# Attention's products with v, from the second query tile on, as float32 with one head in each half of the array's columns

## The chip, the cores and the metric

One core of a Trainium2 chip runs the whole kernel. The metric is the device time of one execution in microseconds. The engines are named as the profile names them: PE (TensorE's matmuls), PEld (its weight loads), DVE (VectorE), ACT (ScalarE), POOL (GpSimd) and SP (the engine whose queue issues most DMAs).

## What is computed

Windowed attention with a distance bias feeds a mixture of four experts, and that feeds one more two-layer network. Cut to what matters:

```python
# q, k, v: (2, 8, 576, 64) float32
scores = np.matmul(q, k.transpose(0, 1, 3, 2)) / np.sqrt(64)
mask = (rel >= 0) & (rel < 128)                  # rel = query - key
scores = np.where(mask, scores + bias, -1e9)     # bias = -slope[h] * |rel|
attn = softmax(scores)
x = np.matmul(attn, v)                           # -> (1152, 512), heads side by side
for e in range(4):                               # w1: 512 x 1024, w2: 1024 x 512
    out += p[:, e:e + 1] * (np.maximum(x @ w1[e], 0) @ w2[e])
h = np.maximum(out @ w_in, 0)                    # w_in: 512 x 2048
return h * h @ w_out
```

## The kernel before

**Rounded products.** Most GEMMs keep float32 accuracy by splitting each operand into a part rounded to float32r (suffix h, written by the helper `rounded`, L519 on ACT or L521 on DVE) and the remainder (suffix l, helper `rest`, L525 on POOL or DVE). A product is then three matmuls: h by h, h by l, l by h. Some early products skip the split and run on plain float32 operands.

**Units.** Attention is cut into units. One unit is a pair of heads c (of four pairs). The first four units take query tile 0 of both batches. The other 16 take one batch and two query tiles: 1 and 2 (256 queries, 384 keys), or 3 and 4 (192 queries, 320 keys, the last block of which has 64). A unit loads q, k and v (tiles rq, rk, rv), splits q and k (qh, ql, khl), and for each query tile does a job: scores (sc, L839), bias and minimum (L852), exponentials (L861), the sums and their reciprocals (L868, L872), scaling of the probabilities in ts (L883, on POOL), four transposes into PSUM (tp, L895), and a copy to SBUF (pt).

**The product with v.** In the first four units pv (L744) multiplies plain float32: each head has 64 columns of v, so its matmul uses 64 of the array's 128 columns, and its result goes to its own 64 partitions of xps. In the other 16 units the probabilities are split: `hi` copies tp to pt rounded, `lo` (DVE) writes the remainder. v is split as well into vh and vl, in fixed tiles that two units in turn share. Then for each of three key blocks pv (L759) runs three matmuls with v of both heads (128 columns) as the weights and the probabilities of both heads side by side as the moving operand:

```python
for l_, r_ in ((wh_, hi), (wh_, lo), (wl_, hi)):
    nc.tensor.matmul(
        out=xps[:, :, o0:o0 + w], lhsT=l_, rhs=r_,
```

Half of that output is of no use (head a's weights with head b's probabilities). `evh` and `evl` take the two useful quarters, 64 partitions by nq columns each, into xh and xl, the split input of the experts.

**Order.** Everything up to 24 items of the first expert's GEMMs is one plan. `Plan.run` is a list scheduler that runs when the program is built: a task has engines to choose from, each with an occupation and a latency, a due time, the tasks it depends on (deps) and the buffers it takes and holds (SLOTS counts the buffers of a kind). It takes the candidate that can start first, and among those that can start within 0.15 of it on the same engine the one with the earliest due time. So a change of a task's cost or its deps can reorder every engine's queue up to the plan's end. `keep_busy` puts small dummy matmuls where the plan sees PE idle near the start. PE's order in the plan mixes the attention units with the first expert's first GEMM (hps, 12 matmuls an item, L974; float32 L1758) and its second (yacc, L1210; float32 L1709). What follows the plan is written out in program order: the rest of expert 0 (hps with 384 columns, L974), then the other experts and the last network (L1093, L1184).

Of the kernel before, what the change touches and what calls it, by code (L numbers as in the profile page):

```python
# [8 lines left out]
F32 = mybir.dt.float32  # L9
F32R = mybir.dt.float32r  # L10
# [6 lines left out]
P = 128  # L17
# [114 lines left out]
def kernel(  # L132
# [346 lines left out]
    def last_runs(nt):  # L479
# [14 lines left out]


    SLOTS = dict(
        rq=3, rk=2, rv=2, qh=2, ql=2, khl=2, vp=2, sc=2, tp=2, ts=5, st=5, pt=2, work=2, y=2, h=4
    )
    plan = Plan(SLOTS)
    actx = ExitStack()  # L500
# [8 lines left out]
    def ps_tile(kind, shape, name):  # L509
        pool = psum[kind][0]  # L510
        psum[kind].append(psum[kind].pop(0))
        return pool.tile(shape, F32, tag=kind, name=name)
# [4 lines left out]
    def rounded(eng, out, in_):  # L517
        if eng == "ACT":
            nc.scalar.activation(out=out, in_=in_, func=ACTF.Copy)  # L519
        else:  # L520
            nc.vector.tensor_copy(out=out, in_=in_)  # L521

    def rest(eng, out, in0, in1):
        e = nc.gpsimd if eng == "POOL" else nc.vector
        e.tensor_tensor(out=out, in0=in0, in1=f32(in1), op=ALU.subtract)  # L525


    def act(n, lat=0.1):
        return ("ACT", 0.1 + 0.00083 * n, 0.1 + 0.00083 * n + lat)

    def dve(n, lat=0.05):
        return ("DVE", 0.15 + 0.00105 * n, 0.15 + 0.00105 * n + lat)

    def gps(n, lat=0.05):
        return ("POOL", 0.2 + 0.0021 * n, 0.2 + 0.0021 * n + lat)

    def pe(us):
        return ("PE", us, us + 0.25)
# [4 lines left out]
    def keep_busy(place):  # L543


        early = plan.at["PE"] < 1.0 and plan.gap > 2.0
        lead, each = (0.6, 0.11) if early else (-0.2, 0.08)
        for _ in range(int(max(plan.gap + lead, 0.0) / each)):
            nc.tensor.matmul(
                out=place, lhsT=idle, rhs=idle, start=True, stop=True, skip_group_check=True  # L550
            )
# [29 lines left out]
                )  # L581

    VS = 3
    vpad = []
    for i in range(2):
        vh = abias.tile([P, VS, 2, D], F32R, name=f"vh{i}")
        vl = abias.tile([P, VS, 2, D], F32R, name=f"vl{i}")
        vpad.append((vh, vl))


    units = [dict(bs=(0, 1), t0=0, t1=1, c=c, col=0) for c in range(NP)]
    for t0, t1, col, n in ((1, 3, 256, 256), (3, 5, 768, 192)):
# [14 lines left out]
    def unit_tasks(u, due):  # L607
# [8 lines left out]


        raw = t0 == 0
        b_ = {k: Buf(k) for k in ("rq", "rk", "rv", "qh", "ql", "khl", "vp", "pt", "work")}
        prev = {k: task.get((k, u - 1)) for k in ("vl", "pv", "evl")}  # L620

        def add(key, opts, fn, **kw):
            task[key, u] = plan.add(f"{key}{u}", opts, fn, **kw)
            return task[key, u]
# [40 lines left out]
        def kl(eng):  # L665
            t = b_["khl"].tile
            rest(eng, t[D:P], b_["rk"].tile, t[0:D])

        parts = [
            (slice(0, r), slice(s0, s1))  # L670
            for r, s0, s1 in ((P, 0, nb * full), (left, full, full + 1)) if r
        ]

        def vsrc():
            return b_["rv"].tile.rearrange("p k (a d) -> p k a d", a=2)

        def vh(eng):
            d["vp"] = vpad[u % 2]
            for r, k in parts:
                rounded(eng, d["vp"][0][r, k], vsrc()[r, k])  # L680

        def vl(eng):
            for r, k in parts:
                rest(eng, d["vp"][1][r, k], vsrc()[r, k], d["vp"][0][r, k])

        end = due[-1]
        first = due[0]
        kbytes = nb * 2 * D * 4 / 1024.0
# [9 lines left out]
        if not raw:  # L698
            tqh = add("qh", [act(G * nq), dve(G * nq)], qh, shared=True, deps=[lq], takes=[b_["qh"]],
                      bufs=[b_["rq"]], due=first - 9.0)  # L700
            tkh = add("kh", [act(G * nk), dve(G * nk)], kh, shared=True, deps=[lk], takes=[b_["khl"]],
                      bufs=[b_["rk"]], due=first - 9.1)
            tql = add("ql", [gps(G * nq), dve(G * nq)], ql, shared=True, deps=[tqh], takes=[b_["ql"]],
                      bufs=[b_["rq"], b_["qh"]], due=first - 8.2)
            tkl = add("kl", [dve(G * nk), gps(G * nk)], kl, shared=True, deps=[tkh],
                      bufs=[b_["rk"], b_["khl"]], due=first - 8.3)
            nv = nb * nk
            tvh = add("vh", [act(nv), dve(nv)], vh, shared=True, deps=[lv], takes=[b_["vp"]],
                      bufs=[b_["rv"]], due=end - 3.4)
            tvl = add("vl", [gps(nv), dve(nv)], vl, shared=True, deps=[tvh], bufs=[b_["rv"], b_["vp"]],  # L710
                      due=end - 2.6)

        split = []
        wide = 0
# [22 lines left out]
        def pv(eng):  # L737

            if raw:
                xps = b_["work"].tile = ps_tile("work", [P, nb * nq], "xps")  # L740
                keep_busy(xps[:, 0:P])
                for i in range(nb):
                    for a in range(2):
                        nc.tensor.matmul(  # L744
                            out=xps[a * D:(a + 1) * D, i * P:(i + 1) * P],
                            lhsT=first_in["v"][:, i, (2 * c + a) * D:(2 * c + a + 1) * D],
                            rhs=b_["pt"].tile[:, 2 * i + a, :], start=True, stop=True,
                            skip_group_check=True,
                        )
                if c == NP - 1:  # L750
                    free.extend(first_buf)
                return
            xps = b_["work"].tile = ps_tile("work", [P, G, nq], "xps")
            keep_busy(xps[:, 0, 0:P])
            for i, (k, r, p0, g, o0, w) in enumerate(mm):
                wh_, wl_ = (x[0:r, k].rearrange("p g d -> p (g d)") for x in d["vp"])
                hi, lo = (b_["pt"].tile[0:r, part, :, p0:p0 + w] for part in range(2))
                for l_, r_ in ((wh_, hi), (wh_, lo), (wl_, hi)):
                    nc.tensor.matmul(  # L759
                        out=xps[:, :, o0:o0 + w], lhsT=l_, rhs=r_,  # L760
                        start=(i == 0 and l_ is wh_ and r_ is hi),
                        stop=(i == len(mm) - 1 and l_ is wl_), skip_group_check=True,
                    )

        cols = slice(d["col"], d["col"] + nb * nq)
# [10 lines left out]
            rest(eng, xl[:, c, cols], first_x[0][0][:, c, :], xh[:, c, cols])  # L776
            x_done()

        heads = [slice(a * D, (a + 1) * D) for a in range(2)]

        def evh(eng):
            for a, hs in enumerate(heads):
                rounded(eng, xh[hs, c, cols], b_["work"].tile[hs, a, :])

        def evl(eng):
            for a, hs in enumerate(heads):
                rest(eng, xl[hs, c, cols], b_["work"].tile[hs, a, :], xh[hs, c, cols])

        us = sum(3 * max(0.112, 0.0135 + 2 * w / 2400.0) for *_, w in mm)
        tpv = add("pv", [pe(0.84 if raw else us)], pv, deps=split + ([lv] if raw else [tvh, tvl]),  # L790
                  takes=[b_["work"]], bufs=[b_["pt"]] + ([] if raw else [b_["vp"]]),
                  due=end - 1.3, follow=[prev["pv"]])
        if raw:
            add("evx", [act(nb * nq), dve(nb * nq)], evx, deps=[tpv], bufs=[b_["work"]],
# [3 lines left out]
            add("evl", [gps(nb * nq), dve(nb * nq)], xl_later, shared=True, deps=[teh],  # L798
                due=end + 7.0)
            return  # L800
        def twice(o):
            return (o[0], 2 * o[1], o[1] + o[2])

        teh = add("evh", [twice(act(nq)), twice(dve(nq))], evh, deps=[tpv], bufs=[b_["work"]],
                  due=end - 0.9)
        add("evl", [twice(dve(nq))], evl, deps=[teh], bufs=[b_["work"]], due=end - 0.4)

    def job_tasks(u, i, t, add, b_, end, ready, G, q0, k0, pos, wide):
        c = units[u]["c"]
# [93 lines left out]
            parts = [(r, k * n, n) for k, r in enumerate(rows)]  # L903

        def hi(eng):
            if raw:
                t_ = b_["pt"].tile = a_tile("pt", [P, 2, 8 * P], F32R).rearrange(
                    "p s w -> p (s w)"
                )[:, 0:G * n].bitcast(F32).rearrange("p (g w) -> p g w", g=G)
                rounded(eng, t_, s["tp"].tile)  # L910
                return
            if i == 0:
                b_["pt"].tile = a_tile("pt", [P, 2, 8 * P], F32R)[:, :, 0:G * wide].rearrange(
                    "p s (g w) -> p s g w", g=G
                )
            for r, o, m in parts:
                rounded(
                    eng, b_["pt"].tile[0:r, 0, :, pos + o:pos + o + m],
                    s["tp"].tile[0:r, :, o:o + m],
                )  # L920

        def lo(eng):
            pt_ = b_["pt"].tile
            for r, o, m in parts:
                rest(
                    eng, pt_[0:r, 1, :, pos + o:pos + o + m], s["tp"].tile[0:r, :, o:o + m],
                    pt_[0:r, 0, :, pos + o:pos + o + m],
                )

        tb = [task["bias", c, True]] + ([task["bias", c, False]] if t else [])  # L930
# [15 lines left out]
        m = G * len(cols) * n  # L946
        thi = stage("hi", [act(m), dve(m)], hi, 2.0, deps=[ttp],
                    takes=[b_["pt"]] if i == 0 else [], bufs=[s["tp"]] + ([b_["pt"]] if i else []))
        if raw:
            return [thi]  # L950
        tlo = stage("lo", [dve(m)], lo, 1.5, deps=[thi], bufs=[s["tp"], b_["pt"]])
        return [thi, tlo]

    state = {}

# [993 lines left out]
```

## Time and profile before

| | before |
|---|---|
| median of 3 runs | 660.81 us (660.63 to 661.75) |
| profiled execution, span from first to last instruction | 658.4 us |
| PE busy | 649.9 us (99%), 3953 matmul records |
| DVE busy | 486.8 us (74%) |
| ACT busy | 320.4 us (49%) |
| POOL busy | 401.7 us (61%) |
| share of PE in the chain that ended last | 89% |
| share of PE xps L759 in it | 3% |

The profile gives the profiled execution's own time only as its span; the runs' times also hold what lies before the first and after the last instruction. A busy PE is one with a matmul in flight; a matmul's record lasts longer than the time after which the next one can start, so costs are read from one row's start to the next row's start. A float32 matmul leaves two records in the trace. The attention units with rounded products lie between 19 and 137 us.

### The profile page before, as it was taken

The numbers are of one execution on the slowest core, as the hardware profiler recorded it, in microseconds if no ns is written. First come the engines' busy times: TensorE is split into PE (matmuls) and PEld (weight loads), VectorE is DVE, ScalarE is ACT, GpSimd is POOL, SyncE is SP. The second block draws the span as 40 slices with busy tenths as digits, with TensorE's granted clock in tenths as the row PEclk, the third lists the DMA queues.
The fourth block names the chain that finished last, engine by engine and source line by source line (L and its number), as shares of the span: only waits on it lengthen the run. The fifth ranks groups of instructions, "written<-read, shape, count | busy, mean of one in ns | idle before, by whom it ended". The sixth has DMA issues, their size and how long they took to land.

```text
span 658.4 us, 11199 instructions
## 1 busy us (share of the span) xinstructions
PE 649.9 (99%) x3953; PEld 582.9 (89%) x3953; DVE 486.8 (74%) x1057; ACT 320.4 (49%) x802; POOL 401.7 (61%) x488
## 2 busy tenths in 40 slices
PE   8999999999999999999999999999999999999998
PEld 7879988889898898998989989989989899898896
DVE  6998977748888768777877876867686676757563
ACT  6998877624454343443344434336545443433320
POOL 1799976509876653654654564445686786665521
PEclk9999999999999999999999999999999999999999
DMA  9952221031313344334334244231113323001012
GB/s 233 271 146 82 65 77 51 11 97 65 109 51 113 128 128 145 127 124 147 100 128 160 80 143 147 81 127 65 34 33 114 126 82 112 1 16 49 1 65 80
DMA packets 44167, 64.44 MB, mean 98 GB/s; under 512 B 4176, under 2 KB 26448, under 8 KB 44112
## 3 DMA queue, kind: packets, MB, share of 16 engines
q1 hardware_dynamic: 32704, 39.22, 19.5%
q10 hardware_dynamic: 11408, 24.51, 11.8%
q8 instruction: 31, 0.51, 0.3%
q14 instruction: 24, 0.20, 0.1%
HBM read 52.97 MB, written 10.75 MB: 97 GB/s over the span
## 4 chain that ended last, share of the span: by engine, by line
PE 89%; POOL 4%; ACT 3%; issue 2%; DMA 2%; DVE 1%; SPq 0%; POOLq 0%; ACTq 0%
PE yacc L1184 34%; PE hps L1093 31%; PE yacc L1210 7%; PE hps L974 6%; PE xps L759 3%; PE tp L895 2%; PE sc L839 2%; POOL hmem L525 1%; PE hps L1758 1%; DMA w<-wconv 1%; ACT ts L861 1%; POOL wl L525 1%; DMA first<-in_qT_dram 1%; PE xtp L1276 1%; POOL ls L525 1%
## 5 line engine op out<-in xcount | busy, mean ns | idle before, releaser
L1184 PE MATMUL yacc<-wh,hmem 128*128 128x512 f32 x716 | 227.8, 390 | 0.0
L1184 PEld LDWEIGHTS yacc<-wh,hmem 128*128 128x128 f32 x716 | 134.5, 188 | 27.1
L1184 PE MATMUL yacc<-wl,hmem 128*128 128x512 f32 x358 | 139.7, 390 | 0.0
L525 POOL TENSOR_TENSOR wl<-wraw,wh 128x256 fp32r<-128x256 f32 (+1 forms) x83 | 79.7, 985 | 39.9 <-ACT wh L458 27.9
L525 POOL TENSOR_TENSOR hmem<-c,hmem 128x320 fp32r<-128x320 f32 (+1 forms) x64 | 59.3, 945 | 60.4 <-ACT hmem L1124 60.4
L525 POOL TENSOR_TENSOR ls<-wsum,hs 128x256 fp32r<-128x256 f32 x77 | 62.1, 834 | 53.2 <-ACT hs L403 52.5
L1104 ACT ACTIVATE p<-hps 128x256 f32<-128x256 f32 (+1 forms) x80 | 32.9, 411 | 108.9 <-PE hps L1093 108.8
L1108 DVE TENSOR_TENSOR u<-hps,p 128x256 f32<-128x256 f32 (+1 forms) x80 | 36.5, 456 | 65.8 <-PE hps L1093 62.8
L1184 PEld LDWEIGHTS yacc<-wl,hmem 128*128 128x128 f32 x358 | 67.3, 188 | 12.5
L525 POOL TENSOR_TENSOR la<-wraw,ha 128x256 fp32r<-128x256 f32 x54 | 49.2, 932 | 17.3 <-ACT ha L389 17.3
L296 DVE SCALAR_TENSOR_TENSOR wconv<-wraw,wconv 128x512 int32<-128x512 int32 x64 | 57.6, 899 | 1.3
L1128 ACT ACTIVATE hmem<-c 128x256 fp32r<-128x256 f32 (+1 forms) x72 | 31.2, 445 | 52.5 <-DVE c L1108 50.7
L1129 DVE SCALAR_TENSOR_TENSOR hmem<-c,hmem 128x256 fp32r<-128x256 f32 (+1 forms) x72 | 42.5, 612 | 14.1 <-ACT hmem L1128 12.7
L1124 ACT ACTIVATE hmem<-c 128x320 fp32r<-128x320 f32 (+1 forms) x64 | 27.3, 446 | 52.4 <-DVE c L1118 33.5
L1093 PE MATMUL hps<-ht,ls 128*128 128x320 f32 (+1 forms) x160 | 47.5, 297 | 1.2 <-POOL ls L525 1.2
L1093 PE MATMUL hps<-ht,hs 128*128 128x320 f32 (+1 forms) x160 | 47.5, 297 | 0.0
L1093 PE MATMUL hps<-xh,hs 128*128 128x320 f32 (+1 forms) x160 | 47.5, 297 | 0.0
L1093 PE MATMUL hps<-xh,la 128*128 128x320 f32 (+1 forms) x160 | 47.4, 296 | 0.0
L1093 PE MATMUL hps<-xl,hs 128*128 128x320 f32 (+1 forms) x160 | 47.4, 296 | 0.0
L1093 PE MATMUL hps<-lt,hs 128*128 128x320 f32 (+1 forms) x160 | 47.4, 296 | 0.0
L1093 PE MATMUL hps<-xh,ha 128*128 128x320 f32 (+1 forms) x160 | 47.3, 296 | 0.0
L1093 PE MATMUL hps<-xl,ha 128*128 128x320 f32 (+1 forms) x160 | 47.3, 296 | 0.0
(157 smaller groups left out, 1732.1 us busy)
## 6 DMA issues: line engine op xcount, KB each, us to landing
wraw<-in_w_dram SPq DMA_DIRECT2D x32, 512.0 KB, 3.7
wraw<-in_w_out_dram ACTq DMA_DIRECT2D x16, 512.0 KB, 3.8
w<-wconv ACTq DMA_DIRECT2D x32, 256.0 KB, 3.9
wraw<-w SPq DMA_DIRECT2D x16, 512.0 KB, 3.3
wraw<-in_w_in_dram ACTq DMA_DIRECT2D x14, 512.0 KB, 3.7
rq<-in_qT_dram SPq DMA_DIRECT2D x8, 256.0 KB, 7.4
out_dram<-y SPq DMA_DIRECT2D x7, 256.0 KB, 2.1
rk<-in_kT_dram SPq DMA_DIRECT2D x8, 192.0 KB, 5.9
```

Of the source, the lines that this page charges most:

```text
L296: nc.vector.scalar_tensor_tensor(out=ai, in0=raw[j][:, :, part], scalar=amount, in1=ai, op0=op, op1=ALU.bitwise_or,)
L525: e.tensor_tensor(out=out, in0=in0, in1=f32(in1), op=ALU.subtract)
L759: nc.tensor.matmul(out=xps[:, :, o0:o0 + w], lhsT=l_, rhs=r_, start=(i == 0 and l_ is wh_ and r_ is hi), stop=(i == len(mm) - 1 and l_ is ...
L974: nc.tensor.matmul(out=ps, lhsT=l_[:, k, cs], rhs=r_[:, k, cols], start=(k == 0 and r_ is xh and l_ is wh and not second), stop=(k == KT - ...
L1093: nc.tensor.matmul(out=ps, lhsT=a[l_][:, k, :], rhs=b[r_][:, k, :], start=start and k == 0 and l_ == r_, stop=stop and k == 1 and l_ == 1, ...
L1104: nc.scalar.activation(out=out, in_=x, func=ACTF.Copy)
L1108: nc.vector.tensor_tensor(out=out, in0=x, in1=y, op=ALU.add)
L1124: nc.scalar.activation(out=hh, in_=r, func=ACTF.Copy)
L1128: nc.scalar.activation(out=hh, in_=src, func=ACTF.Relu)
L1129: nc.vector.scalar_tensor_tensor(out=hl, in0=src, scalar=0.0, in1=f32(hh), op0=ALU.max, op1=ALU.subtract)
L1184: nc.tensor.matmul(out=y, lhsT=l_[:, ns], rhs=r_[:, fo, cols], start=(first and fo == 0 and j == 0), stop=(last and fo == FTQ - 1 and j == 2),
L1210: nc.tensor.matmul(out=y, lhsT=l_[:, ns], rhs=r_[:, fo, :], start=(first and j == 0), stop=(last and j == 2),)
```

## The change

The 16 units from the second query tile on now do what the first four did. v isn't split: the tiles vh and vl, the tasks of that name and their buffers are gone, and pv depends on the load of v (lv). The probabilities aren't split: `hi` copies to a float32 pt, and `lo` is gone. For each key block pv runs two float32 matmuls, one for each head, whose weights are that head's 64 columns of v and whose outputs are that head's 64 partitions; xps is half as large. `evh` and `evl` are one instruction each, on all 128 partitions. rv has 4 buffers in place of 2, pt 3 of half the size in place of 2. The planner's cost of pv is changed.

```diff
     SLOTS = dict(
-        rq=3, rk=2, rv=2, qh=2, ql=2, khl=2, vp=2, sc=2, tp=2, ts=5, st=5, pt=2, work=2, y=2, h=4
+        rq=3, rk=2, rv=4, qh=2, ql=2, khl=2, sc=2, tp=2, ts=5, st=5, pt=3, work=2, y=2, h=4
     )
...
-        def vh(eng):
-            d["vp"] = vpad[u % 2]
-            for r, k in parts:
-                rounded(eng, d["vp"][0][r, k], vsrc()[r, k])
-
-        def vl(eng):
-            for r, k in parts:
-                rest(eng, d["vp"][1][r, k], vsrc()[r, k], d["vp"][0][r, k])
...
-            xps = b_["work"].tile = ps_tile("work", [P, G, nq], "xps")
-            keep_busy(xps[:, 0, 0:P])
+            xps = b_["work"].tile = ps_tile("work", [P, nq], "xps")
+            keep_busy(xps[:, 0:P])
             for i, (k, r, p0, g, o0, w) in enumerate(mm):
-                wh_, wl_ = (x[0:r, k].rearrange("p g d -> p (g d)") for x in d["vp"])
-                hi, lo = (b_["pt"].tile[0:r, part, :, p0:p0 + w] for part in range(2))
-                for l_, r_ in ((wh_, hi), (wh_, lo), (wl_, hi)):
+                for a in range(2):
                     nc.tensor.matmul(
-                        out=xps[:, :, o0:o0 + w], lhsT=l_, rhs=r_,
-                        start=(i == 0 and l_ is wh_ and r_ is hi),
-                        stop=(i == len(mm) - 1 and l_ is wl_), skip_group_check=True,
+                        out=xps[a * D:(a + 1) * D, o0:o0 + w],
+                        lhsT=b_["rv"].tile[0:r, k, a * D:(a + 1) * D],
+                        rhs=b_["pt"].tile[0:r, a, p0:p0 + w], start=(i == 0),
+                        stop=(i == len(mm) - 1), skip_group_check=True,
                     )
...
         def evh(eng):
-            for a, hs in enumerate(heads):
-                rounded(eng, xh[hs, c, cols], b_["work"].tile[hs, a, :])
+            rounded(eng, xh[:, c, cols], b_["work"].tile)
 
         def evl(eng):
-            for a, hs in enumerate(heads):
-                rest(eng, xl[hs, c, cols], b_["work"].tile[hs, a, :], xh[hs, c, cols])
-
-        us = sum(3 * max(0.112, 0.0135 + 2 * w / 2400.0) for *_, w in mm)
-        tpv = add("pv", [pe(0.84 if raw else us)], pv, deps=split + ([lv] if raw else [tvh, tvl]),
-                  takes=[b_["work"]], bufs=[b_["pt"]] + ([] if raw else [b_["vp"]]),
+            rest(eng, xl[:, c, cols], b_["work"].tile, xh[:, c, cols])
+
+        us = 0.19 + sum(4 * max(0.0545, w / 2400.0) for *_, w in mm)
+        tpv = add("pv", [pe(0.84 if raw else us)], pv, deps=split + [lv],
+                  takes=[b_["work"]], bufs=[b_["pt"]] + ([] if raw else [b_["rv"]]),
                   due=end - 1.3, follow=[prev["pv"]])
...
-        if raw:
-            return [thi]
-        tlo = stage("lo", [dve(m)], lo, 1.5, deps=[thi], bufs=[s["tp"], b_["pt"]])
-        return [thi, tlo]
+        return [thi]
```

PE's queue at the product of the first unit with rounded products; before, it stands behind the scores of a later job (xps is the result, pt the probabilities, vh and vl the parts of v):

```order
242 L839 MATMUL sc<-khl,qh 128x256
243 L839 MATMUL sc<-khl,ql 128x256
244 L759 MATMUL xps<-pt,vh_105 128x2x128 x2
245 L759 MATMUL xps<-pt,vl_106 128x2x128
246 L759 MATMUL xps<-pt,vh_105 128x512 x2
247 L759 MATMUL xps<-pt,vl_106 128x512
248 L759 MATMUL xps<-pt,vh_105 128x2x128 x2
249 L759 MATMUL xps<-pt,vl_106 128x2x128
```

The same place after the change, where rv is v as it was loaded:

```order
226 L858 MATMUL tp<-ident,ts 128x128 x4
227 L1654 MATMUL yacc<-wraw,hfirst 128x512 x2
228 L729 MATMUL xps<-pt,rv 64x128 x2
229 L729 MATMUL xps<-pt,rv 64x256 x2
230 L729 MATMUL xps<-pt,rv 64x128 x2
231 L858 MATMUL tp<-ident,ts 128x128 x8
```

Nine matmuls have become six with 64 output partitions each, and the group has moved up, to just behind two float32 matmuls of the second GEMM that follow the unit's last transposes.

The product of the fourth of the 16 units, before; row 331 is another job's four transposes, and the unit's own last transposes stand at row 318, ahead of twelve matmuls of the first GEMM that aren't shown:

```order
331 L895 MATMUL tp<-ident,ts 128x128 x4
332 L839 MATMUL sc<-khl,qh 128x256
333 L839 MATMUL sc<-khl,ql 128x256
334 L839 MATMUL sc<-khl,qh 128x256
335 L839 MATMUL sc<-khl,ql 128x256
336 L1210 MATMUL yacc<-wh,hmem 128x512
337 L1210 MATMUL yacc<-wl,hmem 128x512
338 L1210 MATMUL yacc<-wh,hmem 128x512 x2
339 L1210 MATMUL yacc<-wl,hmem 128x512
340 L1210 MATMUL yacc<-wh,hmem 128x512
341 L759 MATMUL xps<-pt,vh_107 128x2x128 x2
```

The same unit after the change, from its own last transposes (row 312) on:

```order
312 L858 MATMUL tp<-ident,ts 128x128 x4
313 L802 MATMUL sc<-khl,qh 128x256
314 L802 MATMUL sc<-khl,ql 128x256
315 L802 MATMUL sc<-khl,qh 128x256
316 L802 MATMUL sc<-khl,ql 128x256
317 L858 MATMUL tp<-ident,ts 128x128 x4
318 L729 MATMUL xps<-pt,rv 64x128 x2
```

Between the unit's last transposes and its product only four score products and another job's four transposes are left; the second GEMM's six matmuls and the first GEMM's twelve now stand elsewhere.

GpSimd's queue at the start of the rounded units, before:

```order
12 L525 TENSOR_TENSOR ql<-rq,qh 128x512
13 L525 TENSOR_TENSOR vl_106<-rv,vh_105 128x384
14 L883 TENSOR_SCALAR ts<-ts,st_102 128x256 x2
15 L525 TENSOR_TENSOR ql<-rq,qh 128x512
16 L525 TENSOR_TENSOR vl_108<-rv,vh_107 128x384
17 L883 TENSOR_SCALAR ts<-ts,st_98 128x256 x2
18 L883 TENSOR_SCALAR ts<-ts,st_99 128x256 x2
19 L525 TENSOR_TENSOR ql<-rq,qh 128x512
20 L883 TENSOR_SCALAR ts<-ts,st_100 128x256 x2
21 L525 TENSOR_TENSOR khl<-rk,khl 64x768
22 L883 TENSOR_SCALAR ts<-ts,st_101 128x256 x2
```

And after the change:

```order
12 L525 TENSOR_TENSOR ql<-rq,qh 128x512
13 L846 TENSOR_SCALAR ts<-ts,st_102 128x256 x2
14 L525 TENSOR_TENSOR ql<-rq,qh 128x512
15 L846 TENSOR_SCALAR ts<-ts,st_98 128x256 x2
16 L846 TENSOR_SCALAR ts<-ts,st_99 128x256 x2
17 L846 TENSOR_SCALAR ts<-ts,st_100 128x256 x2
18 L525 TENSOR_TENSOR wl<-wraw,wh 128x512
19 L525 TENSOR_TENSOR ql<-rq,qh 128x512
20 L846 TENSOR_SCALAR ts<-ts,st_101 128x256 x2
21 L525 TENSOR_TENSOR wl<-wraw,wh 128x512 x2
```

The remainders of v (vl) are gone, k's remainder (khl) is on DVE, and remainders of weights (wl) have moved up between the scalings of the probabilities.

## Rows read from the trace of the kernel before

**Rows 1.** The page: busy us, share of the span, instructions of each engine.
```profile
PE 649.9 (99%) x3953; PEld 582.9 (89%) x3953; DVE 486.8 (74%) x1057; ACT 320.4 (49%) x802; POOL 401.7 (61%) x488
```
**Rows 2.** Busy time by stretch: PE, PEld, DVE, ACT, POOL, clock, DMA.
```profile
12.00:137.00 125.00, 123.64 (x846) 105.70 (x843) 102.57 (x339) 101.20 (x300) 93.25 (x120) 1.00 0.39 104
137.00:658.00 521.00, 515.98 (x3004) 467.44 (x3002) 377.94 (x670) 212.21 (x475) 306.61 (x359) 1.00 0.29 94
```
**Rows 3.** Waits of PE and PEld, 12 to 137 us: total, times, longest.
```profile
PE tp L895 <- POOL ts L883: 1.0, 1, 1.0
PEld tp L895 <- POOL ts L883: 2.7, 8, 1.2
...
PEld xps L759 <- ACT pt L519: 0.3, 1, 0.3
```
**Rows 4.** PE in order of time: start, us, instruction, idle before.
```profile
45.48 0.28 PE L839 MATMUL sc<-khl,qh 128*128 128x256 f32 x1
45.59 0.28 PE L839 MATMUL sc<-khl,ql 128*128 128x256 f32 x1
46.83 0.89 PE L895 MATMUL tp<-ident,ts 128*128 128x128 f32 x4 [0.96 <-POOL ts L883]
```
**Rows 5.** PE in order of time: a rounded unit with 256 queries.
```profile
36.91 0.40 PE L759 MATMUL xps<-pt,vh 128*128 128x256 f32 x2
...
38.32 0.28 PE L974 MATMUL hps<-xh,wh 128*128 128x256 f32 x1
```
**Rows 6.** PE in order of time: a rounded unit with 192 queries.
```profile
134.97 0.40 PE L759 MATMUL xps<-pt,vh 128*128 128x256 f32 x2
...
135.33 0.51 PE L759 MATMUL xps<-pt,vh 128*128 128x384 f32 x2
135.68 0.33 PE L759 MATMUL xps<-pt,vl 128*128 128x384 f32 x1
135.94 0.44 PE L759 MATMUL xps<-pt,vh 64*128 64x128 f32 x2
...
136.42 0.38 PE L974 MATMUL hps<-xh,wh 128*128 128x256 f32 x1
```
**Rows 7.** PE in order of time: float32 products of the first query tile.
```profile
12.90 0.66 PE L744 MATMUL xps<-pt,first 128*64 128x128 f32 x8
13.49 0.23 PE L549 MATMUL tp<-idle 128*128 128x128 bf16 x1
...
16.65 0.60 PE L1758 MATMUL hps<-xfirst,wraw 128*128 128x256 f32 x2
17.18 1.09 PE L744 MATMUL xps<-pt,first 128*64 128x128 f32 x16
18.20 0.48 PE L1758 MATMUL hps<-xfirst,wraw 128*128 128x256 f32 x1
```
**Rows 8.** PE in order of time: full-width float32 records of 512 columns.
```profile
34.28 1.88 PE L1709 MATMUL yacc<-wraw,hfirst 128*128 128x512 f32 x4
36.00 0.60 PE L895 MATMUL tp<-ident,ts 128*128 128x128 f32 x4
```
**Rows 9.** Groups of the other engines, 12 to 137.5 us: busy us, mean ns.
```profile
L525 DVE TENSOR_TENSOR pt<-tp,pt 128x512 fp32r<-128x512 f32 (+2 forms) x40 | 20.1, 526 | 4.3 <-ACT pt L519 2.9 <-PE sc L839 0.9
L525 DVE TENSOR_TENSOR khl<-rk,khl 64x768 fp32r<-64x768 f32 (+1 forms) x11 | 12.6, 1147 | 0.4
...
L519 ACT ACTIVATE vh<-rv 128x384 fp32r<-128x384 f32 (+2 forms) x20 | 7.8, 419 | 0.2
L525 POOL TENSOR_TENSOR vl<-rv,vh 128x384 fp32r<-128x384 f32 (+2 forms) x24 | 17.7, 748 | 9.6 <-ACT vh L519 7.3 <-PE xps L759 1.8 <-PE tp L895 0.2
```
**Rows 10.** The copy to pt (min/median/max ns), and the exponentials' groups.
```profile
L519 ACT ACTIVATE pt<-tp x40: 257/582/602, 14.7 to 133.7; 128x512 fp32r<-128x512 f32 x23, 128x128 fp32r<-128x128 f32 x7, 64x128 fp32r<-64x128 f32 x7, 128x512 f32<-128x512 f32 x3
L861 ACT ACTIVATE ts<-ts,st 128x256 f32<-128x256 f32 (+2 forms) x69 | 32.8, 479 | 3.6 <-DVE st L852 3.6
L861 ACT ACTIVATION_READ_ACCUMULATOR ts<-ts,st 128x1 f32 (+1 forms) x70 | 13.3, 190 | 0.0
```

More of the change, by code (lines that the diff above doesn't have):

```diff
@@ L583 @@
     VS = 3
[L584 to L588, printed above, removed]
     units = [dict(bs=(0, 1), t0=0, t1=1, c=c, col=0) for c in range(NP)]
@@ L618, in unit_tasks @@
         raw = t0 == 0
-        b_ = {k: Buf(k) for k in ("rq", "rk", "rv", "qh", "ql", "khl", "vp", "pt", "work")}
-        prev = {k: task.get((k, u - 1)) for k in ("vl", "pv", "evl")}
+        b_ = {k: Buf(k) for k in ("rq", "rk", "rv", "qh", "ql", "khl", "pt", "work")}
+        prev = {k: task.get((k, u - 1)) for k in ("pv", "evl")}
         def add(key, opts, fn, **kw):
@@ L667, in kl @@
             rest(eng, t[D:P], b_["rk"].tile, t[0:D])
[L669 to L675, printed above, removed]
-        def vh(eng):
-            d["vp"] = vpad[u % 2]
-            for r, k in parts:
-                rounded(eng, d["vp"][0][r, k], vsrc()[r, k])
-        def vl(eng):
-            for r, k in parts:
-                rest(eng, d["vp"][1][r, k], vsrc()[r, k], d["vp"][0][r, k])
         end = due[-1]
@@ L706, in unit_tasks @@
                       bufs=[b_["rk"], b_["khl"]], due=first - 8.3)
[L707 to L711, printed above, removed]
         split = []
@@ L777, in xl_later @@
             x_done()
-        heads = [slice(a * D, (a + 1) * D) for a in range(2)]
         def evh(eng):
-            for a, hs in enumerate(heads):
-                rounded(eng, xh[hs, c, cols], b_["work"].tile[hs, a, :])
+            rounded(eng, xh[:, c, cols], b_["work"].tile)
         def evl(eng):
-            for a, hs in enumerate(heads):
-                rest(eng, xl[hs, c, cols], b_["work"].tile[hs, a, :], xh[hs, c, cols])
-        us = sum(3 * max(0.112, 0.0135 + 2 * w / 2400.0) for *_, w in mm)
-        tpv = add("pv", [pe(0.84 if raw else us)], pv, deps=split + ([lv] if raw else [tvh, tvl]),
-                  takes=[b_["work"]], bufs=[b_["pt"]] + ([] if raw else [b_["vp"]]),
+            rest(eng, xl[:, c, cols], b_["work"].tile, xh[:, c, cols])
+        us = 0.19 + sum(4 * max(0.0545, w / 2400.0) for *_, w in mm)
+        tpv = add("pv", [pe(0.84 if raw else us)], pv, deps=split + [lv],
+                  takes=[b_["work"]], bufs=[b_["pt"]] + ([] if raw else [b_["rv"]]),
                   due=end - 1.3, follow=[prev["pv"]])
@@ L800, in unit_tasks @@
             return
[L801 to L806, printed above, removed]
+        teh = add("evh", [act(nq), dve(nq)], evh, deps=[tpv], bufs=[b_["work"]], due=end - 0.9)
+        add("evl", [dve(nq)], evl, deps=[teh], bufs=[b_["work"]], due=end - 0.4)
     def job_tasks(u, i, t, add, b_, end, ready, G, q0, k0, pos, wide):
@@ L905, in hi @@
         def hi(eng):
-            if raw:
[L907 to L911, printed above, removed]
             if i == 0:
-                b_["pt"].tile = a_tile("pt", [P, 2, 8 * P], F32R)[:, :, 0:G * wide].rearrange(
-                    "p s (g w) -> p s g w", g=G
+                b_["pt"].tile = a_tile("pt", [P, 8 * P], F32)[:, 0:G * wide].rearrange(
+                    "p (g w) -> p g w", g=G
                 )
@@ L917, in hi @@
                 rounded(
[L918 to L927, printed above, removed]
+                    eng, b_["pt"].tile[0:r, :, pos + o:pos + o + m], s["tp"].tile[0:r, :, o:o + m]
                 )
@@ L948, in job_tasks @@
                     takes=[b_["pt"]] if i == 0 else [], bufs=[s["tp"]] + ([b_["pt"]] if i else []))
-        if raw:
-            return [thi]
-        tlo = stage("lo", [dve(m)], lo, 1.5, deps=[thi], bufs=[s["tp"], b_["pt"]])
-        return [thi, tlo]
+        return [thi]
     state = {}
```

## The prediction

> **What bounds the kernel now.** I read the page's busy shares first: TensorE is busy for 99% of the span [rows 1]. The time by stretches shows whether that holds in the part that is changed: from 12 to 137 us, in which the attention units run, PE is busy 123.64 of 125 us and from 137 us on 515.98 of 521, at a clock of 1.00 (the 2.4 GHz level) in both; VectorE, ScalarE and GpSimd stand at 102.57, 101.20 and 93.25 us in the first stretch [rows 2]. The waits of PE there are small: the matmuls waited 1.0 us and their weight loads 2.7 us for GpSimd's scaled probabilities, the longest wait in each list [rows 3]. The largest single one is at 45.59 us, where the next PE row starts 1.24 us later [rows 4]. So PE's own work sets the end, the three other engines lie beside it, and a microsecond of PE work taken out of the attention units should be a microsecond off the end, unless a new wait takes its place. What follows at 137 us is the same list of instructions in the same order before and after, with no fixed time in it: it moves as a whole.
>
> **What the products cost now.** There are 16 units with rounded products: 8 with 256 queries (tiles 1 and 2) and 8 with 192 (tiles 3 and 4). Each has nine products (three key blocks, three splits). For the first kind, a whole group runs from its first row at 36.91 us to the next work's first row at 38.32 us: 1.41 us [rows 5]. For the second kind from 134.97 to 136.42 us: 1.45 us, although it has fewer columns; the last key block uses only 64 rows of the array, and the rows show what going in and out of that costs: the 384-column product at 135.68 us should take 0.175 us (two of them take 135.33 to 135.68), but the next starts after 0.26 us, and the three small ones take 0.48 us [rows 6]. All 16 together: 8 x 1.41 + 8 x 1.45 = 22.9 us.
>
> **What they will cost.** The first query tile already does its product in the new form, float32 with each head in 64 columns; its rows price the change. A float32 product is two records in the trace, so 8 records are four products of 128 columns. A group of 8 goes from 12.90 us to the next row at 13.49, 0.59 us, and one of 16 from 17.18 to 18.20, 1.02 us [rows 7]. The difference, 8 records in 0.43 us, is 0.054 us a record; the rest, 0.59 - 0.43 = 0.16 us, is paid once, on leaving the half-array form. On entering it, two full-width float32 records of 256 columns take 16.65 to 17.18 us = 0.53 us [rows 7], while four of 512 columns run from 34.28 to 36.00 us [rows 8], 0.215 us for each 256 columns, or 0.43 for two: 0.10 us extra. So 0.26 us for each group.
>
> That 0.054 us also answers the main question, whether the two heads share the array's time: at full width a float32 record of 128 columns costs half of 0.215, 0.108 us; here it costs half of that again. The two heads run side by side.
>
> A first-kind unit becomes 12 records: four of 128 columns, four of 256, four of 128, so 4 x (0.054 + 0.107 + 0.054) = 0.86, with 0.26 it is 1.12 us. The second kind has four each of 128, 192 and 64 columns: 0.22 + 0.32 + between 0.11 (by columns) and 0.22 (no shorter than one of 128), plus the 0.26, plus one more switch to the 64-row form at the 0.09 us that rows 6 show on entry: 1.00 to 1.11 us, and I take 1.07, nearer the upper end since before's 64-row products were also slow for their columns. Sum: 8 x 1.12 + 8 x 1.07 = 17.5 us. **PE's saving is 22.9 - 17.5 = 5.4 us.** Bounds: if the small records go by columns and the 64-row switch costs nothing, 8 x 0.29 + 8 x 0.54 = 6.6 us; if entry, exit and row switch cost half as much again where the neighbours are float32r matmuls (the first tile has float32 and bf16 neighbours only), 16 x 0.13 + 8 x 0.04 = 2.4 us less, 3.0 us.
>
> The Trainium skill, "TensorEngine Tiling (Array Packing)", Key Properties, says that a change of the tiling mode drains the engine, and gives no price; that speaks against a change that makes 16 such round trips. By this trace the drains are the 0.26 us above, 16 x 0.26 = 4.2 us, already in the sum; without them the gain would be 9.6 us. The Trainium skill, "TensorE: Matmul & The Clock Gate", Part 3 (Packing small matmuls), measured 2.38 times for three column tiles, not 3. At that efficiency two tiles would give 1.59 times (an estimate from "TensorE: Matmul & The Clock Gate"), and the column work, 8 x 0.86 + 8 x 0.70 = 12.5 us here, would be 3.2 us more, for a gain of 2.2 us. The first tile's rows show a full 2 at 128 columns and don't agree; wider ones they don't show.
>
> **What goes from the other engines** costs nothing on the path by itself. VectorE loses the 40 remainders of the probabilities (20.1 us) and has 16 xl remainders of full height in place of 32 of half; ScalarE loses its 20 roundings of v (7.8 us); GpSimd the 24 remainders of v (17.7 us) [rows 9]. The planner gives VectorE the five khl remainders that GpSimd had, about 1.1 us each. All three end with less work for a shorter PE, so none becomes the bound. The cover of these edits is PE's 17.5 us and all else that it does; if PE ever stands idle, the relief becomes a gain of its own: the 1.1 us stall at 45.59 us [rows 4], where GpSimd's scaling was late, is the sort of thing that may go.
>
> **The wait that is added.** Before, a unit's product waited for the probabilities' copy and their remainder and for v's two parts; now for the copy and for v's own load. The planner uses the shorter chain to put the product sooner. Between the last transposes and the product PE had 1.4 to 4.2 us of other work; now most units have 1.4 to 2.2 us, but the fourth and eighth of the 16 have only four score products and four transposes, 4 x 0.12 + 4 x 0.108 = 0.91 us (a score product is 0.12 us apart from the next by rows 4's pitch and a transpose is one float32 record). In that time the last transpose must drain and the copy must run, 0.58 us on ScalarE [rows 10], so some 0.9 to 1.0 us is needed: 0 to 0.3 us of wait at two places if ScalarE is free. The score, transposition and GEMM work queued behind on PE waits with it. I set this against the stalls that should go, for a net of zero; -1.5 to +1.5 us is the bound. v's loads have four slots now in place of two and stand earlier in SP's queue relative to need; I cost them at nothing.
>
> **Rivals.**
> 1. The stalls go too: with GpSimd 17.7 us lighter the waits of rows 3 and 4 (1.1, and 2.7 in all) shrink by 1 to 3 us on top: about 653 us. For it: GpSimd's lateness is what PE waits for. Against: GpSimd's queue now takes weight remainders (wl) ahead of the scalings at some places, which may be late again.
> 2. The side-by-side running weakens for the 192- and 256-column records: at half of the benefit 4 x 0.054 x 8 + 4 x 0.040 x 8 = 3.0 us is lost, 658.4 us; with none of it, 6.0 us and no gain left. Only 128 columns are shown.
> 3. Slower: ScalarE's copy stands behind other work in its queue. An exponential of two heads takes 2 x (0.479 + 0.190) = 1.34 us [rows 10] and stands just ahead of the copy in several units. The gain is gone at 5.4 / 16 = 0.34 us a unit and the kernel is measurably slower from 0.42 us; at 0.6 us a unit it would be 660.8 - 5.4 + 9.6 = 665.0 us. For it: the cover fell by half and the remainder no longer pads the chain. Against: PE waited only 0.3 us for a copy before [rows 3], and ScalarE, at 101 of 125 us, gets lighter.
> 4. The change doesn't do what it says, and the heads run one after the other: 8 x 1.98 + 8 x 1.77 = 30.0 us of products (the column work doubled), 7.1 us more than before, 667.9 us. Rows 7 speak plainly against it.
>
> **How the numbers follow.** The profiled span is 658.4 us and the median of the runs 660.81 us, 2.4 us lie around the span; the gain is the same for both. Forecast: 660.8 - 5.4 = 655.4 us, a span of 653.0. Chances: the forecast with its own range of 654.0 to 657.2 us, 0.60; rival 1, 0.17; rival 2, 0.07 (of it 0.05 still faster); waits as in rival 3 that just cancel the gain, 0.07; rival 3 itself, 0.06; rival 4, 0.03. A measurement of this kernel can tell about 0.2%, 1.3 us, from no change. Faster 0.60 + 0.17 + 0.05 = 0.82; same 0.07 + 0.02 = 0.09; slower 0.09. The range that holds 8 in 10 takes in most of rival 1 and the nearer half of rival 2: 653.0 to 658.3 us.
>
> **What would show it.** In the changed profile: the rounded units' groups 1.1 us each from their first row to the next work's, in pairs of records; PE's busy share still 99%; the step from the last attention product to the first 384-column GEMM row about 5.4 us earlier (before: the last group ends at 136.42 us); the stretch after it as long as before. Wrong would be: rows of more than 0.11 us a record at 256 columns (rival 2 or 4); PE waiting for ScalarE's copies for several microseconds (rival 3); or a clock below 1.00 in the attention stage, which no row of before hints at.

## The result and the profile after

The changed kernel takes 654.57 us (median of 4 runs, 653.71 to 654.92) against 660.98 us for the kernel before: a ratio of 0.990, 95% interval 0.9886 to 0.9914. The forecast was 655.4 us, with a range of 653.0 to 658.3.

Busy shares and stretches of the changed kernel; a stretch is given as its bounds, its length, and the busy time of PE, PEld, DVE, ACT and POOL, then clock and DMA. The first stretch goes from the first transposes to the first 384-column GEMM row:

```profile
PE 645.4 (99%) x4001; PEld 574.6 (88%) x4001; DVE 466.7 (71%) x1001; ACT 309.9 (47%) x768; POOL 375.6 (58%) x458
...
11.87:134.41 122.54, 121.24 (x915) 99.00 (x914) 83.03 (x292) 92.16 (x271) 67.84 (x90) 1.00 0.43 110
134.41:653.10 518.69, 513.40 (x2989) 465.37 (x2987) 378.19 (x667) 211.55 (x473) 305.96 (x359) 1.00 0.30 94
```

The same two stretches of the kernel before:

```profile
11.20:139.34 128.14, 126.78 (x866) 108.58 (x866) 104.51 (x348) 102.58 (x305) 93.25 (x120) 1.00 0.40 107
139.34:658.40 519.06, 513.64 (x2989) 465.35 (x2987) 376.81 (x667) 211.64 (x473) 306.61 (x359) 1.00 0.29 93
```

The attention stage is 128.14 - 122.54 = 5.6 us shorter. In it DVE lost 21 us, POOL 25 and ACT 10, and PE is as full as before. What follows has the same length within 0.4 us.

PE in order of time, one group of each kind after the change (start, length with the last record's drain, records); a row begins where the one before lets it:

```profile
34.57 0.28 PE L919 MATMUL hps<-xh,wl 128*128 128x256 f32 x1
34.77 1.09 PE L729 MATMUL xps<-pt,rv 128*64 128x128 f32 x12
35.79 0.70 PE L1654 MATMUL yacc<-wraw,hfirst 128*128 128x512 f32 x1
...
84.92 0.40 PE L1155 MATMUL yacc<-wh,hmem 128*128 128x512 f32 x1
85.25 1.03 PE L729 MATMUL xps<-pt,rv 128*64 128x128 f32 x12
86.21 0.55 PE L858 MATMUL tp<-ident,ts 128*128 128x128 f32 x3
```

The 256-query group takes 34.77 to 35.79 = 1.02 us, the 192-query one 85.25 to 86.21 = 0.96 us, where [rows 5] and [rows 6] had 1.41 and 1.45. The entry shows in the row ahead: 34.57 to 34.77 is 0.20 us, where a matmul of that shape is usually followed after 0.12. All 16 groups together, from start to next row, add to 16.2 us, 0.37 of which are a wait behind the third unit (below); with entries of about 0.10 us each that is 17.8 us, or 17.4 without the wait. Before they add to 23.0.

The waits of PE in the stage (total, times, longest), and the places of the three that are new:

```profile
PE tp L858 <- POOL ts L846: 0.6, 2, 0.3
PE hps L919 <- DVE wl L525: 0.3, 1, 0.3
PE tp L858 <- ACT ts L824: 0.3, 1, 0.3
...
42.67 1.09 PE L729 MATMUL xps<-pt,rv 128*64 128x128 f32 x12
44.07 0.89 PE L858 MATMUL tp<-ident,ts 128*128 128x128 f32 x4 [0.30 <-POOL ts L846]
...
51.92 0.44 PE L858 MATMUL tp<-ident,ts 128*128 128x128 f32 x2 [0.28 <-POOL ts L846]
52.29 1.09 PE L729 MATMUL xps<-pt,rv 128*64 128x128 f32 x12
53.31 0.50 PE L1155 MATMUL yacc<-wh,hmem 128*128 128x512 f32 x1
...
70.63 0.39 PE L919 MATMUL hps<-xh,wl 128*128 128x256 f32 x1 [0.34 <-DVE wl L525]
```

The stall of [rows 4], 1.1 us, is gone, and three of about 0.3 us of idle time stand in its place; the wait for ScalarE's exponentials was there before. The third unit's group isn't slow: it is done at about 43.7 us, and it is the next transposes that wait for GpSimd's scaling. The product of the fourth unit, one of the two with little cover, starts 0.37 us after the start of two transposes; 0.22 us are their columns and 0.10 the entry, so it waited 0.05 us at most for the copy.

GpSimd itself doesn't wait at the first two of these places. Its rows follow each other without idle time from 39.84 to 51.84 us:

```profile
39.84 2.04 POOL L525 TENSOR_TENSOR wl<-wraw,wh 128x512 fp32r<-128x512 f32 x1
41.84 1.28 POOL L525 TENSOR_TENSOR ql<-rq,qh 128x512 fp32r<-128x512 f32 x1
43.09 1.38 POOL L846 TENSOR_SCALAR ts<-ts,st 128x256 f32<-128x256 f32 x2
...
47.63 1.28 POOL L525 TENSOR_TENSOR wl<-wraw,wh 128x512 fp32r<-128x512 f32 x1
48.88 2.98 POOL L846 TENSOR_SCALAR ts<-ts,st 128x256 f32<-128x256 f32 x4
```

The scalings are late because remainders of weights (wl) and of q (ql) stand ahead of them in GpSimd's queue, which the prediction gives as the argument against its rival 1.

### The profile page after: what moved, and what is told of

The parts are those of the page before. It is cut to its first block, busy times and chain, and to the rows that moved or that the text cites. A ratio compares the mean times of both kernels' runs of the same rounds, so it can differ in the third digit from the quotient of the medians.

```text
span 653.1 us, 11154 instructions
## 1 busy us (share of the span) xinstructions
PE 645.4 (99%) x4001; PEld 574.6 (88%) x4001; DVE 466.7 (71%) x1001; ACT 309.9 (47%) x768; POOL 375.6 (58%) x458
## 4 chain that ended last, share of the span: by engine, by line
PE 87%; POOL 6%; issue 3%; DVE 2%; ACT 1%; DMA 0%; POOLq 0%; DVEq 0%; ACTq 0%
PE yacc L1129 34%; PE hps L1038 31%; PE yacc L1155 6%; PE hps L919 6%; PE tp L858 2%; PE xps L729 2%; POOL hmem L525 2%; PE sc L802 2%; PE hps L1703 1%; PE sc L549 1%; POOL wl L525 1%; POOL ts L846 1%; POOL wsum L379 1%; PE xtp L1221 1%; DVE fxwork L955 1%
## 5 line engine op out<-in xcount | busy, mean ns | idle before, releaser
L525 POOL TENSOR_TENSOR wl<-wraw,wh 128x256 fp32r<-128x256 f32 (+1 forms) x82 | 78.1, 976 | 39.9 <-ACT wh L458 28.0
L846 POOL TENSOR_SCALAR ts<-ts,st 128x256 f32<-128x256 f32 (+1 forms) x64 | 32.3, 516 | 33.5 <-DVE st L835 21.2
```

Of the source, the lines that this page charges most:

```text
L846: nc.gpsimd.tensor_scalar(out=ts[0:n, g, :], in0=ts[0:n, g, :], scalar1=st[0:n, 3, g:g + 1], scalar2=1.0, op0=ALU.mult, op1=ALU.mult,)
```

## The experiments

Ratios are to the kernel before, run beside each on the same chip. "The stage" is the first of the two stretches above. The kernel before took 660.45 to 661.05 us beside the experiments, so total times of two of them can be compared to some tenths of a microsecond; the stage is the closer measure.

**Is it the products, or what the other engines no longer do?** One kernel drops the remainders and keeps PE's work:

```diff
-            tvl = add("vl", [gps(nv), dve(nv)], vl, shared=True, deps=[tvh], bufs=[b_["rv"], b_["vp"]],
-                      due=end - 2.6)
...
-                for l_, r_ in ((wh_, hi), (wh_, lo), (wl_, hi)):
+                for j in range(3):
...
+                        out=xps[:, :, o0:o0 + w], lhsT=wh_, rhs=hi, start=(i == 0 and j == 0),
...
-        tlo = stage("lo", [dve(m)], lo, 1.5, deps=[thi], bufs=[s["tp"], b_["pt"]])
```

> The kernel before without the remainders of v and of the probabilities (vl and lo): the three products of a key block all take the rounded parts, so PE's work is the same and the remainders' share of the result is left out. My theory: PE's work sets the end, so only stalls can go, 0 to 2 us: 659 to 661 us. Rival (the relief of VectorE and GpSimd is most of the gain): about 655 us.

Measured: 660.06 us, 0.9994 [0.9985, 1.0003], no change. The other keeps all four parts and changes the products:

```diff
-                        out=xps[:, :, o0:o0 + w], lhsT=l_, rhs=r_,
+                        out=xps[a * D:(a + 1) * D, o0:o0 + w],
+                        lhsT=b_["rv"].tile[0:r, k, a * D:(a + 1) * D],
+                        rhs=b_["pt"].tile[0:r, 0, a, p0:p0 + w], start=(i == 0),
...
```

> The kernel before with only the products in the new form (float32, a head in each half, the planner's cost of them as in the change): v and the probabilities are still split, and the product still waits for all four parts, but reads v and the first copy alone; the evacuations stay in two instructions. My theory: PE's 5.4 us come off, 655 to 656.5 us. Rival (relief): no more than 2 us off, 659 us or more.

Measured: 656.6 us, 0.9938 [0.9926, 0.9951], 0.1 us above what was expected. The stretches, first of the relief alone, then of the products alone:

```profile
11.21:139.30 128.09, 126.29 (x866) 108.92 (x866) 96.58 (x328) 99.51 (x291) 69.27 (x90) 1.00 0.41 107
```

```profile
11.33:135.72 124.39, 121.64 (x914) 99.41 (x914) 107.78 (x350) 105.03 (x313) 88.66 (x110) 1.00 0.40 110
```

With 24 us less on POOL and 8 on DVE (to which the planner gave other work; in the change it loses 21) the stage is as long as before, 128.09 against 128.14 us. PE's idle time in it, the length less the busy time, is 1.8 us against 1.4: the stalls have moved and not gone. With the new products alone the stage is 3.75 us shorter, not 5.6, although the 16 groups are as cheap as in the changed kernel (15.8 us without waits). PE is idle for 2.7 us of it, against 1.3 in the changed kernel, so most of the missing 1.9 us are stalls. The two longest:

```profile
46.69 0.44 PE L894 MATMUL tp<-ident,ts 128*128 128x128 f32 x2 [0.76 <-POOL ts L882]
...
67.82 0.39 PE L838 MATMUL sc<-khl,qh 128*128 128x256 f32 x1 [0.72 <-POOL khl L525]
```

So the relief is worth nothing by itself. Beside the faster products, all else that the change does (the relief, more buffers for rv and pt, evacuations in one instruction, and the order of the queues that follows) is worth about 2 us: it keeps the gain, it doesn't make it. What each of these gives isn't shown; a test below moves the stage by 1.4 us through the order alone.

**Do the two halves run side by side?** Full-width float32 does the same arithmetic without them:

```diff
-                for a in range(2):
+                nc.tensor.matmul(
+                    out=xps[:, :, o0:o0 + w], lhsT=b_["rv"].tile[0:r, k, :],
+                    rhs=b_["pt"].tile[0:r, :, p0:p0 + w], start=(i == 0),
...
```

> The changed kernel with full-width float32 products: both heads' 128 columns of v as weights, both heads' probabilities as the moving operand, half of the output unused as before the change; the evacuations take their two quarters in two instructions again. No change of the array's form but for the 64 rows. My theory: 12 records become 6 of 256, 512, 256 columns, 1.72 us a unit in place of 1.12, and 1.29 plus about 0.2 for the 64 rows in place of 1.06 for the narrower units: 8 x 0.60 + 8 x 0.43 = 8.2 us more, about 662.8 us, so plain float32 without the halves would have lost against the split. Rival (relief of the other engines): about 655 to 656 us.

Measured: 662.93 us, 1.0037 [1.0023, 1.005]. One group of it, PE in order of time:

```profile
34.41 1.89 PE L728 MATMUL xps<-pt,rv 128*128 128x256 f32 x6
36.13 1.88 PE L1656 MATMUL yacc<-wraw,hfirst 128*128 128x512 f32 x4
```

34.41 to 36.13 is 1.72 us, as worked out; three of the eight read 1.53 to 1.54, where the row of a rounded product follows and begins sooner, and the narrower units take 1.58 to 1.61. Without the halves the change would have lost 2.5 us instead of gaining 6.4. The changed kernel's trace shows the two heads directly: of the group at 34.77 us two records have started by 34.80 us, 0.01 us apart, and the next pair starts 0.16 us after the first.

```profile
34.77 0.33 PE L729 MATMUL xps<-pt,rv 128*64 128x128 f32 x2
```

The second test exchanges the loops:

```diff
-            for i, (k, r, p0, g, o0, w) in enumerate(mm):
-                for a in range(2):
+            for a in range(2):
+                for i, (k, r, p0, g, o0, w) in enumerate(mm):
```

> The changed kernel with the two loops of the product exchanged: all three key blocks of head 0, then all of head 1, so that neighbours in PE's queue use the same half of the array; nothing else differs. My theory (the gain is the two heads running side by side): the column work of a unit doubles but for one record at the seam, 0.86 to 1.61 us for 256 queries and 0.70 to 1.29 us for 192, 8 x 0.75 + 8 x 0.59 = 10.7 us more, about 665 us, slower than the kernel before. Rival (the gain is what the other engines no longer do): PE has room, no more than 1 us of change, about 655 us.

Measured: 662.95 us, 1.0037 [1.0024, 1.0051]; slower than before as expected, but for another reason. PE in order of time, a group of each kind:

```profile
34.69 1.36 PE L729 MATMUL xps<-pt,rv 128*64 128x128 f32 x12
35.97 1.99 PE L1654 MATMUL yacc<-wraw,hfirst 128*128 128x512 f32 x4
...
86.27 1.96 PE L729 MATMUL xps<-pt,rv 128*64 128x128 f32 x12
88.15 0.55 PE L858 MATMUL tp<-ident,ts 128*128 128x128 f32 x3
```

The 256-query group takes 1.28 us, not the 1.77 us (1.61 of columns and 0.16 on leaving) of heads that wait for each other: the columns of both heads one after the other would be 1.72 us by themselves, so they still overlap. The records that have started by 35.15 us, by their columns, show how:

```profile
L729 PE MATMUL xps<-pt,rv 128*64 128x128 f32 x4 | 0.7, 298 | 0.0
L729 PE MATMUL xps<-pt,rv 128*64 128x256 f32 x1 | 0.4, 379 | 0.0
```

Head 0 has two records of 128 columns, then two of 256, then two of 128. Four of 128 and one of 256 have started, so two of them are head 1's, ahead of head 0's second record of 256 columns.

The narrower group takes 1.88 us, more than expected. There the heads do run one after the other: up to 87.20 us only head 0's six records have started, and head 1's first starts at 87.21.

```profile
86.27 1.01 PE L729 MATMUL xps<-pt,rv 128*64 128x128 f32 x6
```

What differs there are the 64-row products, of which each head now has its own behind full-row ones, so the form of rows changes twice. That called for a test below.

**What does a change of form cost?** A dummy in the middle of every group:

```diff
+                if i == 1:
+                    nc.tensor.matmul(
+                        out=both[:, 1, 0:P], lhsT=idle, rhs=idle, start=True, stop=True,
...
```

> The changed kernel with one full-width dummy matmul (bf16, 128 columns, 0.056 us, its output unused) behind the first key block of every unit's product, so each group leaves the half-array form and enters it once more. My theory (0.16 us to leave, 0.10 to enter, which the sum took from the first tile): 16 x (0.26 + 0.06) = 5.1 us more, about 659.7 us. Rival (the switch costs next to nothing where products follow one another): 16 x 0.06 = 0.9 us more, about 655.5 us.

Measured: 658.01 us, 0.9960 [0.9945, 0.9975], 3.4 us above the changed kernel. The dummy writes into the same PSUM tile as the products, and the kernel's sums come out changed, so it serves for its times alone. A group of it, PE in order of time:

```profile
34.69 0.44 PE L735 MATMUL xps<-pt,rv 128*64 128x128 f32 x4
35.06 0.23 PE L730 MATMUL xps<-idle 128*128 128x128 bf16 x1
35.22 0.87 PE L735 MATMUL xps<-pt,rv 128*64 128x256 f32 x8
36.02 1.98 PE L1660 MATMUL yacc<-wraw,hfirst 128*128 128x512 f32 x4
```

The group takes 34.69 to 36.02 = 1.33 us, 0.31 more than 1.02, and the 16 of them 5.0 us more, as the price from the first tile says: four records take 0.37 us to the dummy, of which 0.22 are columns and 0.15 the way out. The stage rose by less, to 126.64 us, 4.1 more; PE is idle for 0.8 us of it in place of 1.3, which is the larger part of the difference. The total, 658.01 us, lies below the 659.7 that was expected.

**Does the order of the queues carry the gain?** The planner's old cost of the product:

```diff
-        us = 0.19 + sum(4 * max(0.0545, w / 2400.0) for *_, w in mm)
+        us = sum(3 * max(0.112, 0.0135 + 2 * w / 2400.0) for *_, w in mm)
```

> The changed kernel with the planner's cost of the product as it was before (1.40 and 1.22 us in place of 1.05 and 0.95), so the plan is made for a slower PE and orders the queues otherwise. My theory (PE's work sets the end, the order moves only small stalls): within 1 us of the changed kernel, 653.6 to 655.6 us. Rival (the order that the planner found is a good part of the gain): 657 us or more.

Measured: 655.67 us, 0.9925 [0.9910, 0.9939]: 1.1 us worse by the medians and 1.4 by the stage (123.95 us), a little more than the 1 us that was expected and below the rival's 657 us. Its groups are the same 15.8 us; PE waits 2.2 us for GpSimd's scaling in place of 0.6, at one place 1.2 us:

```profile
PE tp L858 <- POOL ts L846: 2.2, 3, 1.2
...
41.36 0.89 PE L858 MATMUL tp<-ident,ts 128*128 128x128 f32 x4 [1.22 <-POOL ts L846]
```

So the order doesn't make the gain, but another one can cost about a quarter of the stage's 5.6 us.

**Two edits on top.** The 64-row product padded to 128 rows:

```diff
+                for r0 in (0, left):
+                    nc.sync.dma_start(
+                        out=t[r0:r0 + left, full, :], in_=v[b, k0 + full * P:q1, cs]
...
+                e.memset(b_["pt"].tile[r_:P, :, z0:z0 + zw], 0.0)
```

> The changed kernel with the last key block of the 192-query units padded to 128 rows: v's 64 rows are loaded twice, and the 64 rows of the probabilities that belong to the second copy are zeroed, so PE stays in one form of rows; 8 more small DMAs and 8 small memsets. My theory (the switch to 64 rows costs about 0.10 us a unit in the changed profile, 0.256 us from row to row where 0.153 is usual): 8 x 0.10 = 0.8 us less, about 653.8 us. Rival (the memsets and loads cost as much): no change, 654.6 us.

Measured: 652.71 us, 0.9880 [0.9864, 0.9897]. Its narrower groups take 0.81 us where the changed kernel has 0.96, 0.15 us each and 1.2 in all, more than the 0.8 that was expected; the stage is 121.30 us, 1.2 shorter. Two units in one group:

```diff
+            b_["work"].tile = ps_tile("work", [P, 2, nq], "xps")
...
+            mate[2](b_["work"].tile[:, 0, :])
+            products(b_["work"].tile[:, 1, :])
...
+            rounded(eng, xh[:, c - 1:c + 1, cols], b_["work"].tile)
```

> The changed kernel with the products of two neighbouring units (head pairs 0 and 1, or 2 and 3, of the same queries) run as one group into one PSUM tile, evacuated by one instruction of twice the width each for xh and xl; pt has 4 buffers. Half of the entries and exits of the half-array form go. My theory: 8 x 0.26 = 2.1 us less and a little from fewer evacuations, about 652.5 us. Rival (the first unit's buffers are held longer and PE waits for the second): no gain or a loss, 654.6 us or more.

Measured: 652.88 us, 0.9881 [0.9866, 0.9896]; the stage is 120.85 us, 1.7 shorter. The changed kernel again, and beside it the two edits together:

> The changed kernel once more, beside the other two on the same chip, as their reference. Both theories: 654 to 655 us.

Measured: 654.56 us, 0.990 [0.9886, 0.9913]; the profiled span is 651.9 us and the stage 122.6.

> Both of the edits that gained on the changed kernel: products of two neighbouring units in one group, and the last key block of the narrower units padded to 128 rows. My theory (PE's work sets the end, so the two gains add): the stage from the first transposes to the rest of expert 0 was 122.53 us, 121.30 without the 64 rows and 120.85 with two units, so 119.6, about 651.6 us. Rival (stalls of the other engines now set the stage): no better than either edit alone, 652.7 us.

Measured: 651.02 us, 0.9848 [0.9835, 0.9862], the fastest of all. Its stage, and a pair of narrower units in one group:

```profile
11.76:130.87 119.11, 117.80 (x915) 99.31 (x914) 85.60 (x292) 89.21 (x259) 67.32 (x94) 1.00 0.43 111
...
90.31 1.54 PE L736 MATMUL xps<-pt,rv 128*64 128x128 f32 x24
91.78 0.66 PE L884 MATMUL tp<-ident,ts 128*128 128x128 f32 x4
```

119.11 us is 3.4 us below the changed kernel's stage, where the two edits give 1.2 and 1.7 us alone. They more than add, so PE's own work still sets the stage. The extra 0.5 us lies in the narrower pairs, which without the padding look like this:

```profile
89.68 1.98 PE L733 MATMUL xps<-pt,rv 128*64 128x128 f32 x24
91.59 0.66 PE L871 MATMUL tp<-ident,ts 128*128 128x128 f32 x4
```

That is 1.91 us, where the padded pair takes 1.47: 0.44 us, while padding saves 0.30 us on two units by themselves, so 0.14 us more for each of the four pairs. Without the padding the form of rows changes once more in the middle of the pair.

And the heads in turn without the 64-row form:

> The kernel without the 64-row form, with the two heads' products in turn as in heads_in_turn. My theory now (each half of the array takes its own products from the queue, so head 1 starts beside head 0 although it stands behind it; what cost 0.93 us in the narrower units of heads_in_turn was going in and out of the 64-row form twice): groups of about 1.29 and 1.05 us, 8 x 0.27 + 8 x 0.24 = 4.1 us above no_64_rows, 656.8 us. Rival (the heads of a narrower unit do wait for each other): groups of 1.6 us or more there, 661 us.

Measured: 657.12 us, 0.9941 [0.9928, 0.9955], 4.4 us above the padded kernel. A narrower group of it:

```profile
86.27 1.15 PE L732 MATMUL xps<-pt,rv 128*64 128x128 f32 x12
87.35 0.66 PE L871 MATMUL tp<-ident,ts 128*128 128x128 f32 x4
```

1.08 us in place of 1.88. So it was the 64-row form that cost the 0.8 us: without it the heads of a narrower unit overlap as well.

## Why the prediction was right

**PE's work sets the stage.** Shown from both sides: 24 us less on GpSimd moved nothing with the old products, and the edits of PE's work moved the stage by about their size (padding 1.2 us of 1.2, one more switch 4.1 of 5.0). The exception is the products alone, 3.75 of 5.6 us, and there PE was idle for 1.4 us more.

**The price of the new products** came from the first tile's rows and held: 1.12 us with its entry for the wide units (measured 1.02 and 0.10), 1.07 for the narrow ones (0.96 and 0.10). The saving of 5.4 us stands against 23.0 - 17.4 = 5.6 by the groups without the wait in them, and 5.6 by the stage. The 0.16 us that the prediction puts on leaving the form is in two places by the single records: 0.05 us between the first pair and the second, and 0.10 behind the last; the price of a visit is the same. Rivals 2 and 4, less or no overlap, are out: the 256-column records cost what two 128-column ones do, and full width would have cost 662.9 us.

**A term mis-sized.** The switch to 64 rows was put at 0.09 us, what [rows 6] show on the way in. Taking it out saved 0.15 us a unit. The small records, 64 columns each, were put near their upper bound, at 0.18 us for four; in the padded group they go by columns, since 0.22 + 0.32 + 0.11 + 0.16 are the 0.81 us that it takes. That the narrower unit came out at 1.06 us against 1.07 is luck: 0.06 us too little and 0.07 too much.

**The stalls** were set to a net of zero, and by PE's idle time in the stage that was so: 1.4 us before, 1.3 after. But neither half of that sum came. No product waited for ScalarE's copy: at the fourth unit it starts at its usual distance, as shown, and at the eighth too, 0.21 us behind a score product. And the stalls didn't go; they moved to other places, two of them late scalings of GpSimd's and one a weight remainder of VectorE's. That the net held is luck too. I costed the relief of the other engines at nothing; alone it is nothing, yet without it and what came with it 1.9 us of the 5.6 would have been lost, most of it in stalls. Rival 1, a gain from the relief on top, did not come, nor did rival 3, waits for ScalarE's copy.

**What lies outside the sum.** The median fell by 6.4 us, the stage by 5.6. The two profiled executions lie only 658.4 - 653.1 = 5.3 us apart; that of before is the fastest of its four runs, that of the changed kernel the slowest. The time from the start to the first transposes was 11.20 us before, 11.87 and 11.16 us in the two profiles after. Behind the stage the trace of before has one wait of 0.58 us for DVE, at 387.2 to 387.8 us, that neither profile of the changed kernel has, but the first of these has one of 0.51 us at 168.6 to 169.1 us that before lacks. Such waits differ from profile to profile, and some tenths of a microsecond stay open.

## What to carry to other kernels

Where a product has only 64 useful output columns for each of two operands, compare float32 in two halves of the array with a three-way split at full width by records from the same trace: half-array records of 0.054 us per 128 columns, plus 0.26 us for each visit to that form. Gather such products into few, long visits, and pad an odd 64-row block to full rows. A relief of engines that aren't the bound is worth testing together with the edit that speeds up the bound: it was worth 0 alone, and up to 2 us beside it, together with the buffers and the order of the queues that came with it. Look at what stands ahead of the late work in such an engine's queue before you say that it waits.

## What the runs showed of the hardware that was not expected

The two halves of the array don't take their matmuls in the order of the program. With all six records of head 0 ahead of those of head 1, a group took 1.28 us, where six records of one head alone are 0.86 us of columns and twelve in a row 1.72. In the trace's single records head 1's first, of 128 columns, starts at 34.96 us, and head 0's second of 256 columns, which stands ahead of it, at 35.17. The Trainium skill, "TensorE: Matmul & The Clock Gate", Part 3, has matmuls in strict order of the queue; these groups differ from it across column halves.

A change between 128 and 64 rows inside the half-array form costs 0.15 us (0.96 against 0.81 us a group). It also ends the overlap: where each head goes in and out of it by itself, head 1's first record starts 0.15 us after head 0's last, and a group takes 0.8 us more (1.88 against 1.08).
